# Seven products for half of the chunks, in a form with shared operand sums, in place and on one PSUM bank in turn

## The chip, the cores and the metric

The kernel runs on one core of a Trainium2 chip. The metric is device time in microseconds; the time of a kernel is the median of its runs. The engines are called PE (TensorE, the matrix engine), DVE (VectorE), ACT (ScalarE), POOL (GpSimd) and SP (SyncE, which issues the DMAs). PEld is PE's loading of the operand that stays in the array.

## The reference

The program is a linear attention followed by a mixture of four experts.

```python
# attention: r, k, v of (4, 8, 768, 48); batch, heads, time, head size
for t in range(S):
    cur = einsum('bhd,bhe->bhde', u[None] * kt, vt)
    y[:, :, t] = einsum('bhd,bhde->bhe', rt, state + cur)
    state = w[None, :, :, None] * state + einsum('bhd,bhe->bhde', kt, vt)
# ... y becomes x of (3072, 384): 4 * 768 rows, 8 * 48 columns
# experts: w1 of (4, 384, 1024), w2 of (4, 1024, 384), probabilities of (3072, 4)
p = domain_probs / (domain_probs.sum(-1, keepdims=True) + 1e-09)
for e in range(4):
    h = maximum(x @ w1[e], 0.0)
    out += p[:, e:e + 1] * (h @ w2[e])
```

The rows are worked in 24 chunks of 128. Chunk `ci` is time step block `ci // 4` of batch `ci % 4`; four chunks (`SUB`) of one time block form a group `sc`, so there are six groups, 0 to 5.

## The kernel before

The Python program first lists jobs (a piece of work on one engine, with what it needs, the buffers it takes and a rank), then plays them through a small model of the engines in time, and emits each engine's instructions in the order that comes out. So the order on every engine is fixed when the kernel is built, and the durations in the model only decide that order.

Layer 1 multiplies a group's 4 x 128 rows at once: three matmuls of 512 columns for each of 8 blocks (`fb`) of 128 hidden features, and ACT evicts each with a ReLU into `hAll` as bfloat16.

```python
for db in range(NDB):                                  # NDB = 3
    nc.tensor.matmul(ps[:, 0:n, :].rearrange("p a b -> p (a b)"),
                     w1_sb[:, e, db, fb * 128:(fb + 1) * 128],
                     xTe[:, x0 + db, s0:s0 + n, :].rearrange("p a b -> p (a b)"),
                     start=(db == 0), stop=(db == NDB - 1))
# ...
nc.scalar.activation(hTs[:, fb, s0:s0 + n, :], ps[:, 0:n, :], AF.Relu)
```

Layer 2 has two forms. In the groups before `FIRST = 4` (chunks 0 to 15) each chunk and expert has eight matmuls of 384 columns, and the result is weighted with the probability and added up by DVE:

```python
for fb in range(NFB):                                  # NFB = 8
    nc.tensor.matmul(ps, relu_tile(e, sc)[:, fb, s, :], w2_sb[:, e, fb, :],
                     start=(fb == 0), stop=(fb == NFB - 1))
# ...
if e == 0:
    nc.scalar.mul(oacc(ci), tl["o", e, ci], pe)
else:
    nc.vector.scalar_tensor_tensor(oacc(ci), in0=tl["o", e, ci], scalar=pe,
                                   in1=oacc(ci), op0=ALU.mult, op1=ALU.add)
```

From `FIRST` on (chunks 16 to 23) the rows are "scaled ahead": since the probabilities are not negative, p * relu(x w1) = relu((p x) w1), so four copies of a chunk, each times one expert's probability, go into layer 1, and layer 2 is one product over all 4 x 1024 hidden features. A DMA turns the four copies at once.

```python
for e in range(E):
    # on ACT or DVE: y_e[:, e*HD:(e+1)*HD] = Ysb * p_nat[:, e, n_p]
    job(("Xs", ci, e), {"A": 0.61, "V": 0.51}, xs(e), ...)
job(("Xout", ci), {"S": 1.3}, lambda: nc.sync.dma_start_transpose(
    get_xTe(sc)[:, :, ci % B, :], y_e), ...)
```

That product is cut in 2 x 2 blocks: two chunks (`s1`, `s2`), even and odd blocks of hidden features, the two halves of 192 output columns. Seven products of 16 matmuls of 192 columns, in two halves (`hf`) of eight, replace eight. Each product has a PSUM bank of its own for as long as it is evicted; operand sums of `h` go to eight buffers of their own; sums of `w2` are made once, near the end of the plain groups.

```python
SUMS = {1: ((0, s1), (1, s2), ALU.add), 2: ((0, s2), (1, s2), ALU.add),
        5: ((0, s1), (1, s1), ALU.add), 6: ((0, s2), (0, s1), ALU.subtract),
        7: ((1, s1), (1, s2), ALU.subtract)}
# ... for m in (3, 4, 1, 5, 7, 2, 6), for hf in range(2):
nc.vector.tensor_tensor(S, a_of(*x, hf), a_of(*y, hf), op=op)     # 1024 elements
for n in range(8):
    nc.tensor.matmul(tl["P", sc, q, m], st, moving(m, e, i),
                     start=(hf == 0 and n == 0), stop=(hf == 1 and n == 7))
# evictions: products 3 and 4 by an ACT copy into both chunks, product 1 by one
# DVE addition into both, 5, 7, 2 by DVE additions of 192 columns, two for 5 and 2
```

Of the kernel before, what the change touches and what calls it, by code (L numbers as in the profile page):

```python
# [19 lines left out]
def kernel(  # L20
# [65 lines left out]
    spin_in = consts.tile([128, 128], BF16)  # L86
# [27 lines left out]
    RKB = [consts.tile([128, 2, H, P2], BF16, name=f"RK{i}") for i in range(NRK)]  # L114
    for t in RKB:
# [3 lines left out]

    Sbd = [[consts.tile([128, NP, 2 * D], BF16, name=f"S{b}_{i}") for i in range(2)]  # L120
           for b in range(B)]
    for b in range(B):
        for i in range(2):
            nc.vector.memset(Sbd[b][i], 0.0)
    W_sd = [consts.tile([128, H, D], F32, name=f"W{i}_sd") for i in range(2)]
    U_sd = consts.tile([128, H, D], F32)
    wC = consts.tile([128, NP], F32)
    p_nat = consts.tile([128, E, TOTC], F32)
# [8 lines left out]
    GATES = (3, 5, 6, 7, 9, 10, 11, 12)  # L137
# [9 lines left out]
    FIRST = 4  # L147
    LATE, SLOWER = 110.0, {"V": 1.13, "P": 1.06, "A": 1.15}
    SLOTS += [(e, sc, 0) for sc in range(2, FIRST) for e in range(E)]
    ORDER_P = (3, 4, 1, 5, 7, 2, 6)  # L150
    slots = dict(inp=NIN, wst=NST, RKT=4, AtM=2, Ysb=3, ruk=3, dv=3, Vb=4, At=2, tr=1, ys=1,
                 mm=4, xTe=3, hTs=3, oacc=6, Yse=1)
    slots.update({f"{n}{i}": 1 for n, m in (("xTs", 2), ("h", 4), ("S", 8)) for i in range(m)})
# [24 lines left out]

    def spin(n, m=4):

        ps = psum.tile([128, 4, 128], F32, tag="mm", bufs=4, name="spin_ps")
        for _ in range(n):
            nc.tensor.matmul(ps[:, 0:m, :], spin_in, spin_in[:, None, :].to_broadcast((128, m, 128)),
                             start=True, stop=True)
# [10 lines left out]
    def load_in(n, ci):  # L195
        b, c = ci % B, ci // B
        sl = slice(c * C, (c + 1) * C)

        def run():
            t = tl[n, ci] = work.tile([128, H, D], F32, tag=n, bufs=NIN, name=n)  # L200
            nc.sync.dma_start(t, SRC[n][b, :, sl, :].transpose([1, 0, 2]))  # L201
        load_job((n, ci), (0.965, 64), run, (("inp", ci),))

    touched = set()
# [117 lines left out]
    def get_xTe(sc):  # L322
        if ("xTe", sc) not in tl:
            if sc < FIRST:
# [7 lines left out]
    def attention(ci):  # L332
# [7 lines left out]
        if ci >= 2 * SUB:  # L340

            g = GATES[(ci - 2 * SUB) // 2]
            if g < len(SLOTS):
                pre.append(("l1", *SLOTS[g][:2], 0, 0))
            else:
                i, g = divmod(g - len(SLOTS), 8)
                if g < 4:
                    pre.append(("l1", g, FIRST + i, 0, 0))
                else:
                    q, j = divmod((0, 4, 7, 11)[g - 4], 7)  # L350
                    pre.append(("P", FIRST + i, q, ORDER_P[j], 0))

# [10 lines left out]
        for i in range(2):  # L363
# [24 lines left out]
        job(("Vb", ci), {"A": 0.42} if ci < SUB else {"P": 0.5}, vb, [("Vt", ci)],  # L388
# [13 lines left out]
        if dmat:  # L402
# [4 lines left out]
            job(("T", ci, 1), {"S": 1.25}, tr, [("scale", ci, 0), ("scale", ci, 1)], -5.0,  # L407
                (("RKT", ci),), (), (1.1, 64))
            ready = ("T", ci, 1)
        else:  # L410
            two = ci < SUB

            def tr(i):
                def run():
                    if two:
                        tl["T", ci, i] = psum.tile([128, NP, C], BF16, tag=("tr", "At")[i], bufs=i + 1,
                                                   name="RKT_ps")
# [14 lines left out]
            def tout(i):  # L432
                def run(eng):
                    if ("RKT", ci) not in tl:
                        tl["RKT", ci] = work.tile([128, 2, NP, C], BF16, tag="RKT", bufs=4, name="RKT")
                    if parts == 2:
                        copy_on(eng, tl["RKT", ci][:, i], tl["T", ci, i])
                    else:
# [16 lines left out]
        def at():  # L455

            for x in (ci - 1, ci) if paired else (ci,):
                for j in range(2):
                    tag = ("tr", "mm")[j] if paired and x == ci else "At"
                    tl["At", x, j] = psum.tile([128, NP, C], F32, tag=tag, bufs=slots[tag], name="At_ps")  # L460
# [6 lines left out]

        def mk(j):
            def run():
                if j == 0:  # L470
                    tl["AtM", ci] = work.tile([128, 2, NP, C], BF16, tag="AtM", bufs=2, name="AtM")
                nc.vector.tensor_mul(tl["AtM", ci][:, j], tl["At", ci, j],  # L472
                                     mask[:, None, :].to_broadcast((128, NP, C)))
# [9 lines left out]
        for j in range(2):  # L483
            job(("mask", ci, j), {"V": 0.61}, mk(j), [("At", last)],
                rk - 0.5, (("AtM", ci),) if j == 0 else (), ((tags[j], ci, j),),
                behind=(("mask", ci, 0),) if j else ())

        def y():
            ps = tl["Y", ci] = psum.tile([128, H, D], F32, tag="ys", bufs=1, name="Y_ps")
            first = True  # L490
            if c > 0:
                S_now = Sbd[b][c % 2]
# [12 lines left out]
            [("mask", ci, 1), ("Vb", ci)] + ([("S", ci - B)] if c else []), on_pe,  # L505
            (("ys", "Y", ci),), (("AtM", ci), ("Vb", ci), ("RKT", ci)))

        plain = ci < FIRST * SUB

        def yout():  # L510
            if plain:
                tl["Ysb", ci] = work.tile([128, HD], BF16, tag="Ysb", bufs=3, name="Ysb")
# [9 lines left out]
        if dmat and plain:  # L522
            job(("Xout", ci), {"S": 1.2}, lambda: nc.sync.dma_start_transpose(
                get_xTe(sc)[:, :, ci % B, :], tl["Ysb", ci]), [("Yout", ci)], -5.0,
                (("xTe", sc),), (("Ysb", ci),), (0.45, 24))
        elif dmat:
# [11 lines left out]
            for e in range(E):  # L538
                job(("Xs", ci, e), {"A": 0.61, "V": 0.51}, xs(e), [("Yout", ci)] + all_cast, rk - 0.7,
                    (("Yse", ci),) if e == 0 else (), (("dv", ci),), behind=(("Xs", ci, 0),) if e else ())  # L540
            job(("Xout", ci), {"S": 1.3}, lambda: nc.sync.dma_start_transpose(
                get_xTe(sc)[:, :, ci % B, :], y_e),
                [("Xs", ci, e) for e in range(E)] + all_cast, -5.0,
                ((f"xTs{sc % 2}", sc),), (("Yse", ci),), (1.8, 96))
        else:
            tag = "mm" if ci < SUB else "tr"

            def x():
                ps = tl["X", ci] = psum.tile([128, NDB, 128], BF16, tag=tag,
                                             bufs=4 if tag == "mm" else 1, name="xT_ps")  # L550
                for db in range(NDB):
                    nc.tensor.transpose(ps[:, db, :], tl["Ysb", ci][:, db * 128:(db + 1) * 128], ident)  # L552
            job(("X", ci), {"T": 0.17}, x, [("Yout", ci)], on_pe - 1, ((tag, "X", ci),), (("Ysb", ci),))
# [8 lines left out]
        S_now, S_new = Sbd[b][c % 2], Sbd[b][(c + 1) % 2]  # L562
# [9 lines left out]
        def sv():  # L572
            ps = tl["Sp", ci]
            if c:
                a = 1664 + ci % 2 * NP * D
                tl["Tn", ci] = early[:, a:a + NP * D].rearrange("p (q d) -> p q d", d=D)
            for j in range(2):
                pr, cl = slice(j * P2, (j + 1) * P2), slice(j * D, (j + 1) * D)
                wCb = wC[pr, :, None].to_broadcast((P2, NP, D))
                if c == 0:  # L580
                    nc.vector.tensor_mul(S_new[pr, :, cl], ps[pr, :, cl], wCb)
                else:
                    nc.vector.tensor_add(tl["Tn", ci][pr], S_now[pr, :, cl], ps[pr, :, cl])  # L583

        def sp():
            for j in range(2):
                pr, cl = slice(j * P2, (j + 1) * P2), slice(j * D, (j + 1) * D)
                nc.gpsimd.tensor_mul(S_new[pr, :, cl], tl["Tn", ci][pr],  # L588
                                     wC[pr, :, None].to_broadcast((P2, NP, D)))
        job(("Sm", ci), {"T": 0.17}, smm, [("Y", ci), "wC", ("S", ci - B) if c else ("Y", SUB - 1)], on_pe + 1,  # L590
# [3 lines left out]
        else:  # L594
            job(("Sv", ci), {"V": 0.56}, sv, [("Sm", ci)], rk - 0.1, (), (("ys", "S", ci),))
            job(("S", ci), {"P": 1.1}, sp, [("Sv", ci)], rk - 0.5)

    y_e = stg_b[:, 16384:16384 + E * HD]
# [6 lines left out]
    h_free, h_left = [0, 1, 2], {}  # L605

    def h_tag(e, sc):
        return f"h{3 - e}" if sc >= FIRST else "hTs"

    def relu_tile(e, sc):  # L610
        if ("hTs", e, sc) not in tl:
            q = 3 - e if sc >= FIRST else h_free.pop(0)
# [13 lines left out]
    def moe(k, e, sc, single):  # L626
        rk = 10.0 + k
        x0, x_tag = (0, "xTe") if sc < FIRST else (e * NDB, f"xTs{sc % 2}")
        groups = [(fb, 0, SUB) for fb in range(NFB)] if not single else \
            [(fb0, s, 1) for s in range(SUB) for fb0 in (0, 4)]  # L630
        for g, (fb, s0, n) in enumerate(groups):
# [19 lines left out]
            def relu(fb=fb, s0=s0, n=n):  # L651
# [8 lines left out]
                [("Xout", sc * SUB + s) for s in range(s0, s0 + n)] +  # L660
                ([("l2", E - 1, sc * SUB - 1 - s) for s in range(SUB)] if sc == FIRST and e else []) +
                [("S", ci) for ci in range(TOTC - 2 * SUB, TOTC - SUB) if sc == FIRST and not e] +
                [("cast", 1, e, i) for i in pieces_for(fb, nf)], at,
                (("mm", "h", e, sc, fb, s0),) + (((h_tag(e, sc), e, sc),) if sc >= FIRST else ()),
# [3 lines left out]
        if sc >= FIRST:  # L668
            return
        for s in range(SUB):  # L670
# [20 lines left out]
            at = rk + 1 + (s + 0.5) / 4.0  # L691
# [19 lines left out]

    def oacc(ci):
        if ("oacc", ci // 2) not in tl:
            tl["oacc", ci // 2] = big.tile([128, 2, Dm], F32, tag="oacc", bufs=6, name="oacc")
        return tl["oacc", ci // 2][:, ci % 2, :]

    def store(ci, needs, a=0, bb=Dm):
        job(("st", ci, a), {"S": 0.5}, lambda: nc.sync.dma_start(
            out[row0(ci):row0(ci) + C, a:bb], oacc(ci)[:, a:bb]), needs, -6.0, (),
# [7 lines left out]
    def mix(e, what):  # L727
        v = b_of(e)
        B11, B12, B21, B22 = (v[:, :, j, h * DH:(h + 1) * DH] for j in range(2) for h in range(2))
        x, y, op = {1: (B11, B22, ALU.add), 6: (B11, B12, ALU.add), 7: (B21, B22, ALU.add),  # L730
                    3: (B12, B22, ALU.subtract), 4: (B21, B11, ALU.subtract)}[what]
        tag = {6: "Rt", 7: "Kt", 1: "Vt"}.get(what)

        def run(eng):
            if tag:
                o = work.tile([128, H, D], F32, tag=tag, bufs=NIN, name=tag)
                o = tl["mix", e, what] = o.rearrange("p h d -> p (h d)").bitcast(BF16).rearrange(
                    "p (i d) -> p i d", d=DH)
            else:
                o = x  # L740
            (nc.vector if eng == "V" else nc.gpsimd).tensor_tensor(o, x, y, op=op)
        needs = [("cast", 2, e, i) for i in range(NPC)]
        if what in (3, 4):
            needs += [("mix", e, 9 - what if what == 3 else 7)]
            needs += [("l2", e, ci) for ci in range(FIRST * SUB)]
        else:
            needs += [("Vt", TOTC - 1), ("Xout", TOTC - 1)]
# [315 lines left out]
```

## Time and profile before

| | |
|---|---|
| time, median of 3 runs | 292.88 us (292.38 to 293.27) |
| profiled span | 289.4 us |
| L646, L640 | layer 1: 504 matmuls of 512 columns, 288 of 128 |
| L678 | plain layer 2: 512 matmuls of 384 columns |
| L807 | seven products: 448 matmuls of 192 columns |
| L657 | ReLU evictions of 512 columns on ACT: 168, mean 597 ns |
| L689 | weighting and adding on DVE: 48, mean 616 ns |
| L790 | operand sums of `h` on DVE: 40, mean 686 ns |
| L535, L533 | scaling ahead: 19 on DVE, 13 on ACT |

A row "PE out_ps L678 x8" of the chain of work that ended last is a run of eight matmuls of line 678 that write tile `out_ps`, with its start and length in front. `hT_ps` is layer 1, `M_ps` a product, `xTe` the transposed rows, `stg` a staging area for weights that later holds scaled rows and sums. A waits row gives the engine and line that waited, the releaser, the sum in us, the times and the longest. In the 40 slices a digit is the busy share in tenths. Most of layer 2's matmuls of the plain groups stand between layer 1's and the attention's small ones; the last two groups come in clean blocks (layer 1, then products) at the end.

### The profile page before, as it was taken

The numbers are of one execution on the slowest core, as the hardware profiler recorded it, in microseconds if no ns is written. First come the engines' busy times: TensorE is split into PE (matmuls) and PEld (weight loads), VectorE is DVE, ScalarE is ACT, GpSimd is POOL, SyncE is SP. The second block draws the span as 40 slices with busy tenths as digits, with TensorE's granted clock in tenths as the row PEclk, the third lists the DMA queues.
The fourth block names the chain that finished last, engine by engine and source line by source line (L and its number), as shares of the span: only waits on it lengthen the run. The fifth ranks groups of instructions, "written<-read, shape, count | busy, mean of one in ns | idle before, by whom it ended". The sixth has DMA issues, their size and how long they took to land.

```text
span 289.4 us, 6324 instructions
## 1 busy us (share of the span) xinstructions
PE 282.9 (98%) x2482; PEld 181.0 (63%) x2482; DVE 196.2 (68%) x382; ACT 155.8 (54%) x262; POOL 106.0 (37%) x138
## 2 busy tenths in 40 slices
PE   7989999999999999999999999999999999999995
PEld 3777556865955554555555655555544699544995
DVE  5977976797569969674989875554793387120883
ACT  4673968647845243455455466554469701689210
POOL 2875244564979695667567132000000000000000
PEclk9999999999999999999999999999999999999999
DMA  7999999999995898979399556223110001100011
GB/s 152 248 283 271 320 305 269 187 316 202 239 184 112 158 223 191 209 159 179 79 187 194 121 127 111 57 51 60 54 57 0 0 29 40 45 1 2 0 57 54
DMA packets 120418, 40.05 MB, mean 138 GB/s; under 512 B 108458, under 2 KB 120364, under 8 KB 120388
## 3 DMA queue, kind: packets, MB, share of 16 engines
q1 hardware_dynamic: 120372, 39.64, 59.1%
q8 instruction: 19, 0.31, 0.4%
q14 instruction: 11, 0.09, 0.1%
q10 hardware_dynamic: 16, 0.00, 0.0%
HBM read 26.79 MB, written 4.72 MB: 109 GB/s over the span
## 4 chain that ended last, share of the span: by engine, by line
PE 91%; SPq 4%; DMA 3%; issue 0%; DVE 0%; ACT 0%
PE hT_ps L646 38%; PE out_ps L678 28%; PE M_ps L807 13%; PE hT_ps L640 5%; SPq L201 3%; DMA Vt<-in_v_dram 3%; PE At_ps L463 2%; PE Y_ps L501 2%; PE Y_ps L494 1%; PE St_ps L567 1%; SPq L214 1%; DMA xTe<-Ysb 1%; PE RKT_ps L421 1%; PE xT_ps L552 0%; PE p_ps L309 0%
## 5 line engine op out<-in xcount | busy, mean ns | idle before, releaser
L657 ACT ACTIVATE hAll<-hT_ps 128x512 bf16<-128x512 f32 x168 | 99.6, 597 | 73.2 <-PE hT_ps L646 67.7
L678 PE MATMUL out_ps<-w_sb,hAll 128*128 128x384 bf16 x512 | 92.9, 326 | 0.0
L646 PEld LDWEIGHTS <-w_sb 128*128 128x128 bf16 x504 | 46.9, 98 | 49.9 <-DMA xTe<-Ysb 0.8
L646 PE MATMUL hT_ps<-xTe,w_sb 128*128 128x512 bf16 x312 | 77.0, 379 | 0.3 <-DMA xTe<-Ysb 0.3
L678 PEld LDWEIGHTS <-hAll 128*128 128x128 bf16 x512 | 48.6, 98 | 34.0
L689 DVE SCALAR_TENSOR_TENSOR oacc<-out_ps,p_nat,oacc 128x384 f32<-128x384 f32 x48 | 29.4, 616 | 26.2 <-PE out_ps L678 25.6
L646 PE MATMUL hT_ps<-stg,w_sb 128*128 128x512 bf16 x192 | 42.4, 379 | 0.0
L372 POOL TENSOR_TENSOR ruk<-Rt,Kt 128x384 f32<-128x384 f32 x24 | 25.1, 1048 | 30.8 <-DMA Rt<-in_r_dram 17.8
L472 DVE TENSOR_TENSOR AtM<-At_ps,mask 128x512 bf16<-128x512 f32 x48 | 30.7, 681 | 1.4 <-PE At_ps L463 1.3
L398 POOL TENSOR_TENSOR dv<-Vt,dcoef 128x384 f32<-128x384 f32 x24 | 21.3, 889 | 15.3 <-DVE stg L535 7.4
L790 DVE TENSOR_TENSOR RK<-hAll 128x1024 bf16<-128x1024 bf16 x20 | 13.1, 686 | 18.7 <-ACT hAll L657 18.6
L380 POOL TENSOR_TENSOR ruk<-ruk,U_sd 128x384 f32<-128x384 f32 x23 | 25.2, 1097 | 0.8
L588 POOL TENSOR_TENSOR S<-hAll,wC 64x192 bf16<-64x192 f32 x32 | 17.4, 545 | 9.7 <-DVE hAll L583 8.5
L790 DVE TENSOR_TENSOR stg<-hAll 128x1024 bf16<-128x1024 bf16 x20 | 13.1, 686 | 9.7 <-ACT hAll L657 9.5
L640 PE MATMUL hT_ps<-xTe,w_sb 128*128 128x128 bf16 x288 | 18.0, 219 | 0.4 <-ACT w_sb L78 0.2
L640 PEld LDWEIGHTS <-w_sb 128*128 128x128 bf16 x288 | 16.6, 98 | 1.0 <-ACT w_sb L78 0.4
L82 POOL CAST Vb<-Vt 128x384 bf16<-128x384 f32 x20 | 11.6, 581 | 13.6 <-DMA Vt<-in_v_dram 5.3
L359 DVE TENSOR_TENSOR RK<-Kt,W_sd 128x384 bf16<-128x384 f32 x20 | 16.5, 830 | 0.0
L655 ACT ACTIVATE hAll<-hT_ps 128x512 bf16<-128x512 f32 x24 | 14.1, 596 | 4.2 <-PE hT_ps L640 3.3
L687 ACT ACTIVATE oacc<-out_ps,p_nat 128x384 f32<-128x384 f32 x16 | 9.2, 579 | 12.5 <-PE out_ps L678 8.8
L393 DVE TENSOR_REDUCE dcoef<-ruk 128x8 f32<-128x384 f32 x24 | 13.1, 545 | 3.4 <-POOL ruk L380 3.0
L828 ACT COPY oacc<-M_ps 128x384 f32<-128x384 f32 x8 | 3.8, 479 | 19.6 <-PE M_ps L807 19.6
(89 smaller groups left out, 298.4 us busy)
## 6 DMA issues: line engine op xcount, KB each, us to landing
stg<-in_moe_w_dram SPq DMA_DIRECT2D x16, 576.0 KB, 6.6
Kt<-in_k_dram SPq DMA_DIRECT2D x24, 192.0 KB, 3.8
Vt<-in_v_dram SPq DMA_DIRECT2D x24, 192.0 KB, 3.9
Rt<-in_r_dram SPq DMA_DIRECT2D x24, 192.0 KB, 4.3
out_dram<-oacc SPq DMA_DIRECT2D x23, 192.0 KB, 1.9
stg<-in_moe_w_dram SPq DMA_DIRECT2D x8, 384.0 KB, 6.6
RKT<-RK SPq DMA_TRANSPOSE x16, 3.3
out_dram<-oacc SPq DMA_DIRECT2D x2, 96.0 KB, 1.6
```

What stands on the lines that cost most here:

```text
L372: nc.gpsimd.tensor_mul(tl["ruk", ci], tl["Rt", ci], tl["Kt", ci])
L380: nc.gpsimd.tensor_mul(tl["ruk", ci], tl["ruk", ci], U_sd)
L398: nc.gpsimd.tensor_mul(tl["dv", ci], tl["Vt", ci], tl["dcoef", ci].to_broadcast((128, H, D)))
L472: nc.vector.tensor_mul(tl["AtM", ci][:, j], tl["At", ci, j], mask[:, None, :].to_broadcast((128, NP, C)))
L588: nc.gpsimd.tensor_mul(S_new[pr, :, cl], tl["Tn", ci][pr], wC[pr, :, None].to_broadcast((P2, NP, D)))
L640: nc.tensor.matmul(ps[:, i, :], w1_sb[:, e, db, (fb + i) * 128:(fb + i + 1) * 128], xTe[:, db, s0, :], start=(i == 0 and db == 0), stop=(i ...
L646: nc.tensor.matmul(ps[:, 0:n, :].rearrange("p a b -> p (a b)"), w1_sb[:, e, db, fb * 128:(fb + 1) * 128], xTe[:, x0 + db, s0:s0 + n, :].re ...
L657: nc.scalar.activation(hTs[:, fb, s0:s0 + n, :], ps[:, 0:n, :], AF.Relu)
L678: nc.tensor.matmul(ps, relu_tile(e, sc)[:, fb, s, :], w2_sb[:, e, fb, :], start=(fb == 0), stop=(fb == NFB - 1))
L689: nc.vector.scalar_tensor_tensor(oacc(ci), in0=tl["o", e, ci], scalar=pe, in1=oacc(ci), op0=ALU.mult, op1=ALU.add)
L790: lambda S=S, x=x, y=y, op=op, hf=hf: nc.vector.tensor_tensor(S, a_of(*x, hf), a_of(*y, hf), op=op),
L807: nc.tensor.matmul(tl["P", sc, q, m], st, moving(m, e, i), start=(hf == 0 and n == 0), stop=(hf == 1 and n == 7))
```

## The change

The form with seven products starts one group earlier, at group 3 (`FIRST = 3`), and takes another set of sums (four of `h`, four of `w2`, each built upon another). Group 2 (chunks 8 to 11) is scaled ahead too (`SCALED = 2`) and has the plain product, but accumulated over all four experts in one bank, with one eviction. It is for fewer matmul columns, and for fewer evictions on DVE.

```diff
-    GATES = (3, 5, 6, 7, 9, 10, 11, 12)
+    GATES = [3, 4, 9, 4, 5, 6, 6, 24]      # which layer-1 job lets in the attention of chunks 8, 10, ... 22
-    FIRST = 4
+    FIRST = 3
+    SCALED = 2
+    ONTO = {6: 1, 5: 6, 3: 5, 4: 7}        # product -> the product on whose bank it goes on
-    ORDER_P = (3, 4, 1, 5, 7, 2, 6)
+    ORDER_P = (1, 2, 6, 7, 4, 5, 3)
+    SEQ_P = ((0, 1, 0), (0, 2, 0), (0, 7, 0), (0, 1, 1), (0, 2, 1), (0, 7, 1), (0, 6, 0), (0, 6, 1), (0, 4, 0),
+             (1, 1, 0), (0, 5, 0), (0, 5, 1), (0, 4, 1), (1, 1, 1), (0, 3, 0), (0, 3, 1), (1, 2, 0), (1, 2, 1),
+             (1, 7, 0), (1, 7, 1), (1, 6, 0), (1, 6, 1), (1, 4, 0), (1, 5, 0), (1, 5, 1), (1, 4, 1), (1, 3, 0),
+             (1, 3, 1))                     # (pair of chunks, product, half) in PE's order
+    EARLY_P = 6                            # the first half product may start before the last layer-1 block
...
```

The sums of `h` are in place, and wait for the product that still reads the old value:

```diff
+                o, x, y, op = {1: (None, A21, A22, ALU.subtract), 3: (A21, A21, A11, ALU.subtract),
+                               2: (A11, None, A11, ALU.subtract), 4: (A12, A12, A11, ALU.add)}[k]
+                nc.vector.tensor_tensor(o, x, y, op=op)
+            if k in (2, 4):
+                needs += [("P", sc, q, 1 if k == 2 else 2, h) for h in hs]
```

For the first pair of chunks they are done in halves (1024 elements), for the second pair whole (2048). A product in `ONTO` starts without resetting its bank, once the earlier sum in it has been copied out:

```diff
+                if m in ONTO:
+                    tl["P", sc, q, m] = tl["P", sc, q, ONTO[m]]
+                ...
+                    nc.tensor.matmul(tl["P", sc, q, m], st, moving(m, hf, n),
+                                     start=(hf == 0 and n == 0 and m not in ONTO), stop=(hf == 1 and n == 7),
+                                     skip_group_check=True)
+            if m in ONTO:
+                needs = needs + [("C", sc, q, ONTO[m])]
...
+                    if first:                      # products 1, 6, 7, 3
+                        nc.scalar.copy(o, ps)      # 192 columns
+                    else:                          # products 2, 5, 4
+                        nc.vector.tensor_add(o, o, ps)
```

Chunks 8 to 11, and the transposes of the scaled rows in two halves:

```diff
+            job(("l2s", ci, e), ...)       # 4 experts x 8 matmuls of 384 columns, one bank
+        job(("evs", ci), {"A": 0.48}, lambda: nc.scalar.copy(oacc(ci), tl["o", ci]), ...)
...
-            job(("Xout", ci), {"S": 1.3}, lambda: nc.sync.dma_start_transpose(
-                get_xTe(sc)[:, :, ci % B, :], y_e),
+            for hf in range(2):
+                job(("Xout", ci, hf), {"S": 1.25}, lambda hf=hf: nc.sync.dma_start_transpose(
+                    get_xTe(sc)[:, 2 * NDB * hf:2 * NDB * (hf + 1), ci % B, :],
+                    y_e[:, 2 * HD * hf:2 * HD * (hf + 1)]),
```

Four sums of `w2` (each over two experts, 1536 elements) are written to output buffers and to buffers of the transposed rows that are no longer used, and one in place. Some pairs of attention operations become one: the scaling of k and r (from chunk 8 on), the mask of even chunks from 8 on, the addition of the state; the state's two buffers a batch become one. The rest of the diff moves buffers to make room.

## The prediction

> **What bounds the kernel now.** I read the page first: the busy shares and the 40 slices, then the chain.
>
> ```profile
> PE 282.9 (98%) x2482; PEld 181.0 (63%) x2482; DVE 196.2 (68%) x382; ACT 155.8 (54%) x262; POOL 106.0 (37%) x138
> ...
> PE   7989999999999999999999999999999999999995
> PEld 3777556865955554555555655555544699544995
> DVE  5977976797569969674989875554793387120883
> ...
> PEclk9999999999999999999999999999999999999999
> ...
> PE 91%; SPq 4%; DMA 3%; issue 0%; DVE 0%; ACT 0%
> ```
>
> After the first tenth of the span TensorE (PE) is never idle for a visible part of a slice, at full clock, and the chain that ended last is 91% PE; the rest is the loading at the start and the last store. "Busy" alone doesn't prove it, since matmul ends are modelled, so I took the spacing of the matmuls from the chain in order of time and the durations by form:
>
> ```profile
> 167.37 1.30 PE out_ps L678 x8
> ...
> 212.50 16.19 PE hT_ps L646 x75
> 228.68 18.48 PE M_ps L807 x224
> 247.16 20.72 PE hT_ps L646 x96
> 267.88 18.50 PE M_ps L807 x224
> ```
>
> The start-to-start gaps are 1.30/8 = 162.5 ns at 384 columns, 18.48/224 = 82.5 ns at 192 columns, 20.72/96 = 215.8 ns at 512 columns. The last 77 us are three blocks of back-to-back matmuls. So a microsecond is won only by issuing fewer columns, or lost by making PE wait. The waits of PE in the whole trace are under 1.2 us each, and after 30 us there is one:
>
> ```profile
> PE hT_ps L646 <- DMA xTe<-Ysb: 0.3, 1, 0.3
> ```
>
> By the time-line it is at 109.8 us: the first layer of chunks 8 to 11 stands ready for the transposed activations just as they land (0.75 us for the weight load). That is the tightest hand-over there is, and the change lengthens it.
>
> ```profile
> 80.00:110.00 30.00, 29.74 (x241) 16.71 (x239) 23.96 (x45) 11.80 (x21) 23.88 (x29) 1.00 0.86 167
> 110.00:155.00 45.00, 45.00 (x360) 25.31 (x359) 35.11 (x68) 22.49 (x40) 27.96 (x38) 1.00 0.84 171
> 155.00:212.00 57.00, 57.00 (x413) 31.46 (x412) 37.59 (x71) 31.02 (x54) 8.72 (x12) 1.00 0.43 91
> ```
>
> The columns are stretch, length, busy us of PE, PEld, DVE, ACT, POOL, clock, DMA share, GB/s. Around 80 to 110 us DVE and POOL are 80% busy and DMA 86%: this is where new attention work could make PE late. ACT is 39% busy there.
>
> **What the Trainium skill says.** (1) TensorE: Matmul & The Clock Gate, Wait — 56ns, not 53.3ns?: warm back-to-back matmuls start N / 2.4 GHz plus about 2.5 ns apart. That gives 82.5, 162.5 and 215.8 ns for 192, 384 and 512 columns, which are the gaps above. The form with seven products doesn't pay less per column than the plain one except for that 2.5 ns. (2) PSUM — Partial Sum Buffer, The four PSUM rules: the first matmul of a group resets a bank, those without that flag add to what is there, and a read in the middle of a group is allowed if synchronised. The new accumulation "in turn" relies on it; no run so far shows its timing. (3) VectorE: DVE Perf Modes, Side-by-side: a bf16 two-operand operation makes two results a cycle with some 158 cycles of fixed cost at 0.96 GHz: 698 ns for 1024 elements and 965 ns for 1536. The trace has 686 ns for the 1024-wide sums, so it agrees within 2%.
>
> **The change part by part.** Durations are the means of the groups of instructions by form: eviction with weight and addition (L689) 616 ns, scaling on DVE (L535) 432, on ACT (L533) 606, sum (L790) 686, output addition (L822) 352 and over two chunks (L834) 554, mixed weights (L741) 551, scaled copy of an expert's output (L687) 579, copy of a product (L828) 479.
>
> *PE.* Chunks 12 to 15 leave the plain second layer and take the seven products. Removed: 4 chunks x 4 experts x 8 = 128 matmuls of 384 columns, 128 x 162.5 ns = 20.80 us. Added: 2 pairs x 7 products x 16 = 224 matmuls of 192 columns, 224 x 82.5 ns = 18.48 us. Net -2.32 us. Chunks 16 to 23 had seven products already and have seven still. Chunks 8 to 11 keep 128 matmuls of 384 columns; that they now accumulate over four experts in one bank changes no column. The first layer and the attention matmuls are unchanged. So the sum for PE is -2.3 us, all on the path, because PE is the path.
>
> *DVE.* Removed: the evictions of 8 chunks with three experts each, 24 x 616 ns = 14.8 us. Scaling ahead moves from 8 to 16 chunks: 64 scalings instead of 32 (19 of these were on DVE at about 430 ns, 13 on ACT at 606 ns); in the same ratio that adds 19 x 0.43 = 8.2 us to DVE and 13 x 0.61 = 7.9 us to ACT. Sums: now 40 halves x 0.686 = 27.4 us for four pairs; then 24 halves (16.5) plus 12 full ones that I estimate at 1.22 us from (3) (14.7), 31.2 us for six pairs: +3.8. Output additions: 24 x 0.352 + 4 x 0.554 = 10.7 us now, 6 x 3 x 0.352 = 6.3 after: -4.4. Mixed weights: 20 x 0.551 = 11.0 us become 8 of 1536 elements, about 0.96 each: -3.3. The merged scale, mask and state operations save fixed costs only, about 0.2 us each on some 40: some -6. Together about -16 us, to some 180 us. None of it is on the path.
>
> *ACT.* It loses 8 scaled copies (4.6 us) and the 8 copies of 479 ns (3.8), and gains 7.9 us of scaling, 4 copies of whole chunks (1.9) and 24 of 192 columns at about 0.33 us (7.9): about +9, to some 165 us, still under 60% of the span.
>
> *DMA and SP.* The scaled transposes of chunks 8 to 11 and 12 to 15 carry four blocks instead of one. Now a plain one lands 2.7 us and a scaled one 3.7 us after issue; after, two issues of half size for each chunk. This is bandwidth in a stretch that is 84 to 86% busy.
>
> *Hand-overs inside the products.* Product 6 goes onto product 1's bank after ACT has copied it; then 5, then 3; 4 goes onto 7. The order of issue puts other halves between: from the end of product 1 to the start of 6 are 2 halves of 8 x 82.5 = 0.66 us, 1.32 us, against a copy of 0.33 us and a hand-over of 0.2 to 0.3. From 5 to 3 there is one half, 0.66 us, against an addition of 0.35. It fits, with little to spare. The sums in place follow the same pattern: the last first-layer eviction ends some 0.9 us after the last first-layer matmul; the sum left over from the first half, then two sums for the second half take 3 x 0.69 us, so the sum for product 7 is ready at about 3.0 us, and PE needs it after five halves, at 3.3 us. I allow 0.07 us for each of the three groups of chunks, 0.2 us in all; more than that is rival B.
>
> *End.* The last addition by DVE (0.35 us) becomes an ACT copy of about the same length, before the same half store. No change.
>
> *Start of chunks 8 to 11.* Each chunk now needs four scalings (about two rounds of 0.5 us, on two engines) and a transpose that lands 1 us later: 2 us more, at the place where PE waited already. Against it the attention of chunks 10 to 15 is let in earlier, and the second layer of chunks 4 to 7 can stand in between. I call it even, with the present wait of 0.75 us neither gone nor grown; a worse hand-over is rival A.
>
> Sum: 292.9 - 2.3 + 0.2 + 0 = 290.8 us, 0.7% less. The start of chunks 8 to 11 is the weakest term, since it is a judgement and no sum.
>
> **The rivals.**
>
> *A. PE waits for scaled activations at about 107 us.* For: the hand-over above, DMA at 86%, POOL and DVE at 80%. Against: ACT is 39% busy there and can take half of the scalings, 16 x 0.61 us over 30 us. If the attention isn't early enough, PE loses 3 to 8 us: 293 to 298 us.
>
> *B. The chain of sums and copies in place sets the pace of the products.* For: the kernel before writes its sums to eight separate buffers and each product to a bank of its own, so nothing there had to wait for a product to be read; now a sum waits for a product, the product for the sum, and the next for a copy. Against: the interleaved order. If each of six pairs lost 1 us, the time would be 296 us, slower than before.
>
> *C. The schedule gains more than the columns.* DVE loses 16 us and the evictions of four experts become one. If that freed PE, the time would fall to 286 us. Against: PE showed one wait after 30 us, so there is nothing to free.
>
> *D. Only the columns count:* 292.9 - 2.3 = 290.6 us. This is what I believe.
>
> **Range and chances.** D gives 290.6, the allowance makes it 290.8. A moderate case of A or B adds 3 us, the lucky one takes off 2: 288.8 to 294.0 for 8 in 10. Faster by over 2% would be under 287.0, which needs 3.6 us that PE doesn't show as waiting: 6%. Slower by over 2% is over 298.7, A and B at full size together: 6%. Within 2%: 88%.
>
> **What would show it right or wrong.** Right: 672 matmuls into M_ps at 82.5 ns, 384 into out_ps, PE busy near 281 us, three blocks of products of 18.5 us each, no PE wait on DVE or ACT over 0.5 us in them. A shows as a wait of PE on a transposing DMA into the staging area near 110 us. B shows as product blocks of more than 19 us and waits of the M_ps matmuls on DVE sums or ACT copies. Wrong in its core would be a block of 224 products that costs more than 82.5 ns a matmul without a wait, or a span that falls by over 4 us. DVE near 180 us and ACT near 165 us test the accounts beside the path.

## The result and the profile after

| | before | after |
|---|---|---|
| time, median of 4 runs | 293.07 us (292.38 to 293.43) | 290.08 us (288.98 to 290.90) |
| ratio | | 0.9898 (95% interval 0.9858 to 0.9938) |
| profiled span | 289.4 us | 288.3 us |

The change makes the kernel 1.0% faster, 3.0 us by these medians, and the interval leaves out 1; measured again beside other kernels the ratio was 0.9911 (0.9880 to 0.9942). The page after, with engines' busy time, the slices, and the chain that ended last by engine:

```profile
PE 280.0 (97%) x2558; PEld 187.4 (65%) x2578; DVE 182.0 (63%) x305; ACT 168.8 (59%) x300; POOL 106.7 (37%) x127
...
PE   8989999999999899999999999999999999999995
DVE  4977877687759777858553897788417473010760
...
PEclk9999999999999999999999999999999999999999
...
PE 81%; SPq 6%; DMA 6%; DVE 3%; ACT 2%; issue 1%; POOL 0%; DVEq 0%; ACTq 0%
```

PE is as full as before, apart from the 14th slice (94 to 101 us). The chain in order of time shows the products (M_ps) in three places:

```profile
185.50 2.64 PE M_ps L904 x32
...
188.69 6.71 PE M_ps L904 x80
...
195.77 3.96 PE M_ps L904 x48
...
200.10 5.30 PE M_ps L904 x64
...
227.52 18.48 PE M_ps L904 x224
...
266.72 18.49 PE M_ps L904 x224
```

In groups 4 and 5 all 224 matmuls run in 18.48 us, 82.5 ns apart as before, although they now share banks and their sums are in place. Group 3's stand in four pieces with attention between them, and these add up to 2.64 + 6.71 + 3.96 + 5.30 = 18.61 us: 0.13 us is lost there. In the groups by form M_ps has 672 matmuls and out_ps 384. The longest wait of PE after the start, and the part of the chain that leads to it:

```profile
PE hT_ps L706 <- DVE o_sb L748: 1.0, 1, 1.0
```

```profile
82.61 5.08 DMA RKin<-in_k_dram
...
93.58 4.41 DMA stg<-stg
98.02 0.42 DVE stg L590
98.44 0.46 DVE Tn L635
98.91 1.13 DVE AtM L523
100.04 0.54 DVE o_sb L748
100.62 0.81 PE hT_ps L706 x3
```

Read from the bottom: layer 1 waited for a PSUM bank, which DVE freed late (L748 is the weighting of an expert's output), because DVE, which keeps its order, had stood before a scaling (L590) until a transposing DMA had read the buffer it writes. The matmuls that waited belong to the last expert of chunks 4 to 7. Layer 1 of chunks 8 to 11, where the prediction looked for a wait, starts at 116 us straight behind layer 2 of the group before:

```profile
110.95 5.20 PE out_ps L737 x32
116.15 0.21 PE hT_ps L706
```

The windows of the prediction, after:

```profile
80.00:110.00 30.00, 28.82 (x250) 16.99 (x251) 22.84 (x39) 16.83 (x31) 19.09 (x23) 1.00 0.93 162
110.00:155.00 45.00, 44.84 (x322) 24.87 (x324) 30.91 (x46) 28.07 (x51) 21.81 (x25) 1.00 0.83 166
155.00:212.00 57.00, 56.74 (x521) 38.82 (x525) 39.94 (x61) 32.76 (x63) 21.20 (x25) 1.00 0.68 133
```

PE lost 1.2 us of 30 in the first stretch; the later dents are mostly matmul records missing from the trace (484 of 504 matmuls into hT_ps are in it). In the profile of the repeated measurement that wait is absent, and the span is 287.1 us.

### The profile page after: what moved, and what is told of

Same layout as the page of the kernel before. It is cut to its first block, busy times and chain, and to the rows that moved or that the text cites. A ratio compares the mean times of both kernels' runs of the same rounds, so it can differ in the third digit from the quotient of the medians.

```text
span 288.3 us, 6434 instructions
## 1 busy us (share of the span) xinstructions
PE 280.0 (97%) x2558; PEld 187.4 (65%) x2578; DVE 182.0 (63%) x305; ACT 168.8 (59%) x300; POOL 106.7 (37%) x127
## 4 chain that ended last, share of the span: by engine, by line
PE 81%; SPq 6%; DMA 6%; DVE 3%; ACT 2%; issue 1%; POOL 0%; DVEq 0%; ACTq 0%
PE hT_ps L706 34%; PE M_ps L904 19%; PE out_ps L737 11%; PE out_ps L967 7%; PE hT_ps L700 4%; SPq L229 4%; DMA stg<-in_moe_w_dram 2%; DMA RKin<-in_k_dram 2%; DMA stg<-stg 2%; SPq L246 1%; PE Y_ps L553 1%; PE At_all L506 1%; PE Y_ps L546 1%; SPq L243 1%; DVE stg L590 1%; PE St_ps L626 1%
## 5 line engine op out<-in xcount | busy, mean ns | idle before, releaser
L706 PE MATMUL hT_ps<-stg,w_sb 128*128 128x512 bf16 x372 | 85.4, 379 | 0.6
L904 PEld LDWEIGHTS <-hAll 128*128 128x128 bf16 x576 | 47.6, 98 | 0.8
L737 PE MATMUL out_ps<-w_sb,hAll 128*128 128x384 bf16 x256 | 45.7, 326 | 0.3 <-POOL w_sb L82 0.3
L406 POOL TENSOR_TENSOR ruk<-RKin 128x384 f32<-128x384 f32 x24 | 26.8, 1118 | 45.5 <-DMA RKin<-in_k_dram 26.5
L737 PEld LDWEIGHTS <-hAll 128*128 128x128 bf16 x256 | 24.1, 98 | 15.3 <-issue 0.4
L706 PE MATMUL hT_ps<-xTe,w_sb 128*128 128x512 bf16 x112 | 28.8, 379 | 1.5 <-DVE o_sb L748 1.0
L645 POOL TENSOR_TENSOR S<-Tn,wC 64x192 bf16<-64x192 f32 x32 | 23.6, 737 | 11.1 <-DVE Tn L635 9.9
L904 PE MATMUL M_ps<-w_sb,hAll 128*128 128x192 bf16 x288 | 26.5, 246 | 0.0
L590 DVE TENSOR_SCALAR stg<-dv,p_nat 128x384 bf16<-128x384 f32 x36 | 20.9, 610 | 5.6 <-DMA stg<-stg 5.5
L967 PE MATMUL out_ps<-w_sb,hAll 128*128 128x384 bf16 x128 | 22.0, 326 | 0.0
L748 DVE SCALAR_TENSOR_TENSOR o_sb<-out_ps,p_nat,o_sb 128x384 f32<-128x384 f32 x24 | 14.6, 615 | 11.4 <-PE out_ps L737 11.4
L588 ACT ACTIVATE stg<-dv,p_nat 128x384 bf16<-128x384 f32 x28 | 16.7, 610 | 7.1 <-DMA stg<-stg 6.2
L967 PEld LDWEIGHTS <-hAll 128*128 128x128 bf16 x128 | 12.1, 98 | 7.7
L394 DVE TENSOR_TENSOR RK_sb<-RKin,W_both 128x768 bf16<-128x768 f32 x16 | 16.7, 1061 | 0.5 <-DMA RKin<-in_k_dram 0.5
```

The costliest lines, as they stand in the source:

```text
L394: job(("scale", ci, 0), {"V": SCALE_US}, lambda: nc.vector.tensor_mul(RK[:, :, :, 0:D], tl["in", ci], W_both), [("Rt", ci), ("Kt", ci), (" ...
L406: nc.gpsimd.tensor_mul(tl["ruk", ci], tl["Rt", ci], tl["Kt", ci])
L590: nc.vector.tensor_scalar(o, tl["Ysb", ci], scalar1=p_nat[:, e, n_p:n_p + 1], scalar2=None, op0=ALU.mult)
L645: nc.gpsimd.tensor_mul(S_new[pr, :, cl], Tn2[pr, tn_at[ci], :, cl], wC[pr, :, None].to_broadcast((P2, NP, D)))
L904: nc.tensor.matmul(tl["P", sc, q, m], st, moving(m, hf, n), start=(hf == 0 and n == 0 and m not in ONTO), stop=(hf == 1 and n == 7), skip_ ...
L967: nc.tensor.matmul(tl["o", ci], relu_tile(e, sc)[:, fb, s, :], w2_sb[:, e, fb, :], start=(e == 0 and fb == 0), stop=(e == E - 1 and fb == ...
```

## The experiments

Theory: only the matmul columns count, 2.3 us for each group that takes seven products. Rivals: the relief of DVE or the new order makes the gain (C); the hand-over of banks and sums in place costs PE time (B). Twelve runs, each timed against the kernel before on the same chip. Products: the number of groups with seven products. Not all runs shared a chip, so two rows are best compared by their ratios.

| kernel | products | median us | ratio to before (95%) |
|---|---|---|---|
| after_again | 3 | 289.05 | 0.9911 (0.9880 to 0.9942) |
| plain_g3 | 2 | 292.07 | 1.0000 (0.9978 to 1.0022) |
| products_g2 | 4 | 292.27 | 1.0019 (0.9995 to 1.0043) |
| unscaled_g2 | 3 | 299.71 | 1.0266 (1.0228 to 1.0304) |
| products_g2_order | 4 | 288.72 | 0.9902 (0.9878 to 0.9927) |
| order_only | 3 | 288.99 | 0.9904 (0.9876 to 0.9932) |
| unscaled_g2_gate | 3 | 289.70 | 0.9931 (0.9908 to 0.9954) |
| no_weave | 3 | 307.77 | 1.0563 (1.0522 to 1.0603) |
| pool_beside | 3 | 289.83 | 0.9941 (0.9914 to 0.9967) |
| products_g2_act | 4 | 286.99 | 0.9827 (0.9788 to 0.9865) |
| act_order_only | 3 | 288.68 | 0.9915 (0.9886 to 0.9944) |
| products_g2_act_again | 4 | 286.55 | 0.9835 (0.9806 to 0.9864) |

**after_again.** No edit.

> The changed kernel again, beside the others on the same chip. All theories: 0.986 to 0.994 of the time before, about 290 us.

As expected: 0.9911.

**plain_g3: take the columns back, keep all else.**

```diff
-    FIRST = 3
+    FIRST = 4
```

> Group 3 (chunks 12 to 15) takes the plain product accumulated over four experts instead of seven products; all else stays. Theory of columns: 224 matmuls of 82.5 ns become 128 of 162.5 ns, so 2.3 us more than the changed kernel, 0.997 to 1.000 of the time before. Rival, the gain comes from relieving DVE of evictions and from the new schedule: less than 1 us more than the changed kernel, since both stay.

Measured: the time of the kernel before, and 3.0 us above after_again, which ran on the same chip. Its busy times:

```profile
PE 283.3 (98%) x2482; PEld 181.3 (63%) x2482; DVE 167.4 (58%) x289; ACT 165.9 (57%) x294; POOL 103.5 (36%) x127
```

DVE does 29 us less than in the kernel before (196.2), PE the same 283 us, and the time hasn't moved. Relief of DVE and the new order are worth nothing by themselves, taken together and within the interval of 0.6 us either way. That rules out rival C, and the gain of the change is that of its columns. The 14 times of plain_g3 lie in two heaps, 290.3 to 291.2 us (six) and 292.0 to 292.8 (eight), for no reason that the record shows; so the 3.0 us are uncertain by more than their digits say.

**unscaled_g2 and unscaled_g2_gate: take only the scaling ahead of group 2 back.**

```diff
-    SCALED = 2
+    SCALED = 3
# and in unscaled_g2_gate besides
-    GATES = [3, 4, 9, 4, 5, 6, 6, 24]
+    GATES = [3, 4, 9, 4, 5, 6, 6, 20]
```

> Group 2 (chunks 8 to 11) is not scaled ahead: four evictions a chunk on ACT and DVE again (12 more additions on DVE, 7.4 us), 16 scalings fewer, small transposes. No matmul column changes. Theory of columns: within 1 us of the changed kernel, and 1 us of it downwards if the wait of PE at 100 us goes. Rival, the relief of DVE is part of the gain: 1.5 us or more slower than the changed kernel.

> As unscaled_g2, but the attention of chunks 22 and 23 is let in by the same layer-1 job as in the changed kernel (the number that names it had shifted, and PE waited 8 us for their transposed rows). Theory of columns: within 1 us of the changed kernel. Rival, the relief of DVE is part of the gain: 1.5 us or more slower than the changed kernel.

The first missed, by an oversight in the edit: a gate is a position in the list of layer-1 and product jobs, and `SCALED` shifts those positions, so chunks 22 and 23 were let in too late. The longest wait of PE in its trace shows it:

```profile
PE hT_ps L706 <- DMA stg<-stg: 7.9, 1, 7.9
...
253.53 4.87 PE L706 MATMUL hT_ps<-stg,w_sb 128*128 128x512 bf16 x11 [7.93 <-DMA stg<-stg]
```

The run is 10.7 us slower than after_again, more than it waited. The second row, from the time-line, shows the rest: eleven matmuls of 512 columns took 4.87 us, about twice the gap of 215.8 ns. The granted clock fell to 0.50 during the wait and was back at about 259.3 us; by estimate that costs half of the 5.8 us from 253.5 on, 2.9 us. In all five executions the mean clock was 0.983 to 0.988.

With the gate set right the time is 289.70 us, 0.65 us from after_again, within the 1 us that columns alone allow; the two intervals leave 1.1 us either way, so the rival's 1.5 us is unlikely rather than excluded. DVE is busy for 181.7 us there and for 180.9 in after_again: the additions came back, but the scalings went. So the run tests the form of group 2 and not the relief of DVE, which plain_g3 tests. The form of group 2 is not where the gain is.

**no_weave: the same work with PE's order not interleaved.**

```diff
+    SEQ_P = tuple((q, m, h) for q in (0, 1) for m, h in ((2, 0), (2, 1), (1, 0), (7, 0), (7, 1), (1, 1), (6, 0),
+             (6, 1), (5, 0), (5, 1), (3, 0), (3, 1), (4, 0), (4, 1)))
```

> The same products, sums and copies as the changed kernel, but PE runs each pair by itself and products 6, 5 and 3 follow directly on the product whose bank they go on. If the hand-over in a bank costs the copy (0.32 us) and two signals (0.2 us each), three hand-overs a pair and six pairs make some 12 us, and product 7 waits for its sum besides: 12 to 20 us slower than the changed kernel, 1.03 to 1.06 of the time before. Rival, the hand-over is short enough to vanish in the pipeline of PE: less than 2 us slower.

Measured: 18 to 19 us slower than the changed kernel, inside the expected 12 to 20. The waits of PE, and one hand-over of a bank in time (start, length, engine and line):

```profile
PE M_ps L902 <- DVE hAll L871: 7.7, 6, 1.5
PE M_ps L902 <- ACT o_sb L923: 3.7, 9, 0.4
PE M_ps L902 <- DVE o_sb L925: 2.8, 6, 0.6
```

```profile
281.81 0.82 PE L902 MATMUL M_ps<-w_sb,hAll 128*128 128x192 bf16 x8
...
282.68 0.32 ACT L923 COPY o_sb<-M_ps 128x192 f32<-128x192 f32 x1 [0.34 <-PE M_ps L902]
...
283.05 0.82 PE L902 MATMUL M_ps<-o_sb,hAll 128*128 128x192 bf16 x8 [0.41 <-ACT o_sb L923]
```

At the gap of 82.5 ns PE could have started the next matmul at 281.81 + 8 x 0.0825 = 282.47 us. The copy starts 0.21 us later and takes 0.32, and product 6 starts 0.05 us after its end: 0.58 us in all. In the interleaved order PE has at least one half product, 0.66 us, in each such place, and two or more in most. So rival B's cost is real, and the order of the change hides it: in groups 4 and 5 nothing of it is left. The parts were not as expected, though. Some 12 us were put on the banks; the rows give them 3.7 + 2.8 = 6.5 us of waiting, and 7.7 us to the sums in place.

**products_g2: the next group.**

```diff
-    FIRST = 3
+    FIRST = 2
```

> Group 2 (chunks 8 to 11) takes the seven products too. Theory of columns: another 2.3 us less than the changed kernel, about 0.982 of the time before. Rival: the sums of the weights must be ready some 20 us earlier and the sums of h fall among the attention of later chunks; if DVE becomes late there, PE waits for it and the time stays at 0.990 or rises.

Measured: 3.2 us slower than after_again instead of 2.3 faster. The stretch of group 2's products and what PE waits for there:

```profile
140.00:160.00 20.00, 17.27 (x193) 15.93 (x191) 17.85 (x25) 8.68 (x19) 13.07 (x13) 0.91 0.65 118
```

```profile
146.43 1.85 DVE L873 TENSOR_TENSOR stg<-hAll 128x2048 bf16<-128x2048 bf16 x1
...
148.21 0.54 DVE L568 TENSOR_TENSOR dv<-Y_ps,dv 128x384 f32<-128x384 f32 x1
...
148.81 0.34 PE L626 MATMUL St_ps<-Vb,RK_sb 128*128 128x96 bf16 x4 [1.02 <-DVE dv L568]
...
151.01 1.25 PE L904 MATMUL M_ps<-w_sb,stg 128*128 128x192 bf16 x8 [0.54 <-DVE w_sb L817]
```

DVE is busy for 17.85 of 20 us (third pair of numbers), PE for only 17.27. A sum of 2048 elements holds up an attention operation, and PE waits for that. The expected rival came true.

The wait cost more than its length, as in unscaled_g2. From 148 to 150 us PE was busy for 0.34 us of 2; then the granted clock fell, to 0.91 over this stretch (the number after the pairs) and to 0.50 from 152 to 154 us. Eight matmuls of 192 columns before and after:

```profile
146.96 0.82 PE L904 MATMUL M_ps<-w_sb,hAll 128*128 128x192 bf16 x8
...
152.37 1.48 PE L904 MATMUL M_ps<-w_sb,stg 128*128 128x192 bf16 x8
```

The mean clock of 0.994 over 292.3 us makes an estimated 1.7 us. Of the 22 executions 19 show 0.988 to 0.994, of the kernel before 4 of 77; the three at full clock took 291.0 to 291.2 us, still 2 us above after_again. So part of the 3.2 us is the clock, and the rest are waits, 2.7 us of them in this stretch.

**products_g2_order and order_only.** The sums of `w2` are made earlier and the gates moved; order_only has the same without group 2's products.

```diff
-    GATES = [3, 4, 9, 4, 5, 6, 6, 24]
+    GATES = [4, 4, 9, 3, 6, 4, 24, 19]
-    MIX_RANK = 18.0
-    XS_ON = {'A': 0.61, 'V': 0.51}
-    VB_ON = {'A': 0.42, 'P': 0.5}
-    XS_RANK = 0
-    SUM_RANK = -60
+    MIX_RANK = 15.5
+    XS_ON = {'A': 0.61, 'V': 0.65}
+    VB_ON = {'P': 0.5}
+    XS_RANK = 2
+    SUM_RANK = -30
# and FIRST = 2 in products_g2_order alone
```

> Seven products for group 2 too (chunks 8 to 23), and another order: the sums of the weights are ranked before the last attention chunks, the last attention chunks are let in at other points, DVE's scaling is listed as dearer and the copies of v go to POOL alone. Theory: products_g2 lost its 2.3 us to waits of PE for DVE between 147 and 155 us; without those it should show 2.0 to 2.6 us less than the changed kernel, 0.980 to 0.985 of the time before. Rival, DVE is too full among the attention of groups 3 and 4 in any order: the time stays at 0.99 or above and the waits turn up elsewhere.

> The other order of products_g2_order alone, with seven products for chunks 12 to 23 as in the changed kernel. Theory of columns: within 0.6 us of the changed kernel. Rival, what products_g2_order may gain comes from the order: 1.5 us or more faster than the changed kernel.

order_only is at the time of the changed kernel, as expected. products_g2_order missed: it gains 3.5 us on products_g2 (its mean clock was 0.999 or more), but not the 2.3 on the changed kernel, so the rival came true. DVE then PE, in time:

```profile
144.72 2.02 DVE L872 TENSOR_TENSOR stg<-hAll 128x2048 bf16<-128x2048 bf16 x1
146.66 0.55 DVE L567 TENSOR_TENSOR dv<-Y_ps,dv 128x384 f32<-128x384 f32 x1
```

```profile
147.26 0.34 PE L545 MATMUL Y_ps<-S,RKT 128*128 128x96 bf16 x4 [0.91 <-DVE dv L567]
```

The sum takes 2.02 us here; the same form takes 1.22 us in groups 4 and 5. The places where it is long are those where POOL works.

**pool_beside: POOL made busy beside group 4's products.**

```diff
+            if j.name == ("dv", 23):
+                for _ in range(60):
+                    nc.gpsimd.tensor_mul(U_sd, U_sd, U_sd)
```

> The changed kernel with 60 operations of 384 elements added on POOL after its last own work (U_sd times itself, not used again), so that POOL is busy from about 203 to 263 us: beside the products of group 4 and not beside those of group 5. If DVE's bf16 sums are slowed by work of POOL, as products_g2_order suggests (a sum of 1024 elements 0.69 us where POOL is idle, 1.0 to 1.5 us where it is busy), the sums of group 4 take 0.8 to 1.5 us and those of group 5 stay at 0.69, and PE may wait in group 4: 0 to 4 us more in all. Rival, they were long for another reason (order, reads of h beside PE): both groups at 0.69 and the time of the changed kernel.

Measured: DVE beside busy POOL (group 4), and in the same run without it (group 5):

```profile
228.30 1.31 DVE L873 TENSOR_TENSOR stg<-hAll 128x1024 bf16<-128x1024 bf16 x1
...
231.99 0.34 DVE L927 TENSOR_TENSOR o_sb<-o_sb,M_ps 128x192 f32<-128x192 f32 x1
...
234.46 1.84 DVE L873 TENSOR_TENSOR stg<-hAll 128x2048 bf16<-128x2048 bf16 x1
```

```profile
268.28 0.68 DVE L873 TENSOR_TENSOR stg<-hAll 128x1024 bf16<-128x1024 bf16 x1
...
270.40 0.34 DVE L927 TENSOR_TENSOR o_sb<-o_sb,M_ps 128x192 f32<-128x192 f32 x1
...
271.87 1.22 DVE L873 TENSOR_TENSOR stg<-hAll 128x2048 bf16<-128x2048 bf16 x1
```

The sums from SBUF to SBUF go from 0.68 to 1.31 us and from 1.22 to 1.84 (of group 4's eight short ones one kept 0.69 us, the others took 1.1 to 1.3); the output addition, with one operand in PSUM, stays at 0.34. PE waited 1.0 us for a sum in group 4; the medians differ by 0.8 us from after_again's, with intervals that overlap. The Trainium skill agrees, SBUF — State Buffer, Who interferes with whom: a DVE instruction with two SBUF inputs contends with a GpSimd instruction that reads SBUF, and one with a single SBUF input outside the two-port modes does not.

**products_g2_act, act_order_only and products_g2_act_again: take work from DVE and POOL in that stretch.**

```diff
-    GATES = [3, 4, 9, 4, 5, 6, 6, 24]
+    GATES = [6, 3, 9, 7, 10, 7, 6, 18]
-    MIX_RANK = 18.0
-    XS_ON = {'A': 0.61, 'V': 0.51}
-    VB_ON = {'A': 0.42, 'P': 0.5}
-    XS_RANK = 0
-    SUM_RANK = -60
+    MIX_RANK = 15
+    XS_ON = {'A': 0.61}
+    VB_ON = {'A': 0.42}
+    XS_RANK = 1
+    SUM_RANK = -30
-    EARLY_P = 6
+    EARLY_P = 5
-            ... {"V": 1.26 if hf == 2 else 0.74}, run, needs,
+            ... {"V": (1.26 if hf == 2 else 0.74) * {2: 1.5, 3: 1.4}.get(sc, 1.0)}, run, needs,
# FIRST = 2 in products_g2_act, FIRST = 3 in act_order_only
```

> Seven products for chunks 8 to 23 again, with less for DVE and POOL beside group 2's and 3's products: all scaling ahead and the copies of v from chunk 8 on go to ACT, sums of groups 2 and 3 are listed as 1.5 and 1.4 times as dear, and the last attention chunks are let in at other points. If the 2.3 us were lost to DVE alone, about 0.984 of the time before; if ACT with 92 more operations of some 0.5 us takes DVE's place as the one PE waits for, 0.99 or above with waits for ACT.

> The settings of products_g2_act (scaling and copies of v on ACT, dearer sums, other points of entry) with seven products for chunks 12 to 23 only, as in the changed kernel. Theory of columns: 2.3 us more than products_g2_act, close to the changed kernel, 0.989 to 0.994 of the time before. Rival, the settings brought the gain: within 0.8 us of products_g2_act.

> products_g2_act beside act_order_only on the same chip: 0.980 to 0.986 of the time before, 2.0 to 2.6 us less than act_order_only.

Measured: 0.9827 and 0.9835, and without group 2's products 0.9915, so 2.1 us (288.68 to 286.55) for that group. The same 20 us, first of products_g2_order, then of products_g2_act:

```profile
140.00:160.00 20.00, 19.09 (x247) 18.27 (x245) 18.77 (x27) 7.27 (x18) 13.74 (x14) 1.00 0.62 118
```

```profile
140.00:160.00 20.00, 20.00 (x244) 18.97 (x242) 14.94 (x24) 10.05 (x24) 5.54 (x7) 1.00 0.46 100
```

DVE falls from 18.77 to 14.94 us, POOL from 13.74 to 5.54, and PE waits no more. The settings were changed together, so which of them, less for DVE or less for POOL beside it, made the room is not shown. This kernel beats both: 1.7% below the kernel before, 0.8% below the changed one.

## Why the prediction was right

*The size.* 290.8 us was predicted and 290.08 measured; in shares of the time before, 0.7% less was predicted and 1.0% measured, with 0.7% inside the interval. The term that carries it, -2.3 us of columns, was shown by taking it back: the time of the kernel before returned. Of the four pairs that differ by one group and nothing else, two gave 3.0 us (plain_g3 to after_again) and 2.1 (act_order_only to products_g2_act_again); where DVE was too full, one gave 0.3 (order_only to products_g2_order) and one a loss of 3.2 (after_again to products_g2). Whether the first change is 2.3 or 3.0 us can't be told: each ratio has an interval of some 0.6 to 1.2 us either way, and the profiles of plain_g3 and after_again, by the start of group 4's products (228.15 and 226.27 us), say 1.9.

*The gaps between matmuls.* 82.5 ns held in the products. (The prediction calls the last 77 us three blocks; its rows show four, over 73.9 us. The argument doesn't hang on it.) Of the three blocks of 18.5 us that it expected after the change, groups 4 and 5 are such blocks, and group 3 takes its 18.6 us in four pieces.

*DVE, ACT.* DVE was to fall to some 180 us and is at 182.0, ACT to rise to 165 and is at 168.8. That DVE's sum came so close is partly luck. The scalings took 20.9 us instead of the 16.4 reckoned (36 of 610 ns on average, and from 0.40 to 1.16 us in after_again; the prediction's 432 ns is the busy time shared out, where the profile before has a mean of 462), and the merged attention operations saved some 9 us instead of 6. ACT also took over copies of v (15 instead of 4, 5.6 us more), which the prediction left out. Nothing of it showed in the time, as said; plain_g3 shows that a fall of 29 us doesn't either.

*Hand-overs in the products.* 0.2 us was allowed; 0.13 us is to be seen in group 3 and nothing in groups 4 and 5. The cost assumed for one, 0.33 us for the copy and 0.2 to 0.3 for the signals, was measured as 0.58 us where it isn't hidden.

*Start of group 2.* It was called even, with the wait of 0.75 us neither gone nor grown. It is gone: layer 2 of the group before stands in between, which the prediction named as a way out. But the root it feared, scaled rows whose transpose is late, cost PE about 1 us at another place, 15 us earlier in layer 1 of chunks 4 to 7, in the profiled run and not in the repeat. And there DVE waited for the DMA, and PE for DVE. So "even" was right for the sum, not for the path.

*Rival C* was dismissed for the right reason. *Rivals A and B* were each real costs that this order of the schedule covers: no_weave pays 18 us for B, and unscaled_g2 pays for scaled rows that come late, at group 5 and not at 107 us. What products_g2 pays for, too full a DVE beside the attention, the prediction had as neither.

*What the prediction missed.* It took a sum's time for fixed. That holds in the products of groups 4 and 5, where POOL has nothing left to do, and would have misled for one group more. It also took the clock for full throughout. That held for the change, and not in products_g2 and unscaled_g2.

## What to carry to other kernels

Where one engine is full from end to end at a known gap, count its instructions, and take relief of other engines at zero until the trace shows a wait for them. Work that is taken off the full engine is collected only if the helpers can feed it there: the same edit gave -2.1, -0.3 or +3.2 us according to what else DVE and POOL had to do in those 20 us. And count a long wait of the full engine as more than its length, if the clock falls after it. Sharing one PSUM bank among products in turn costs nothing if more than the copy and its signals (0.58 us here) of other matmuls stands between.

## What the runs showed of the hardware that was not expected

bf16 additions on DVE with both operands in SBUF took 0.68 to 0.69 us (1024 elements) and 1.22 us (2048) beside an idle POOL, and up to 1.31 and 1.84 us beside POOL's tensor products in pool_beside (2.02 in products_g2_order), while an addition with one operand in PSUM kept its 0.34 us. POOL pays too: its 60 products took 0.83 us at the median and up to 1.69 us.

The granted clock fell to 0.50 for some microseconds after PE had been nearly or wholly idle (busy for 0.34 of 2 us in products_g2, a wait of 7.9 us in unscaled_g2). In no_weave, whose waits of up to 1.5 us have full work between them, and in the changed kernel it is 0.9 or more in every slice of the span. How long PE must be idle for it, no run shows, and four executions of the kernel before had a mean of 0.993 or 0.994 too.
